# Blocks 5 to 15 of a dense layer taken in pairs, with 512-column first products

## The chip, the core and the metric

The kernel runs on one core of a Trainium2 chip. TensorE (PE, with its weight loads PEld), VectorE (DVE), ScalarE (ACT), GpSimd (POOL) and SyncE (SP, which issues most DMAs) run their own queues in order and wait for one another by semaphores. The metric is device time in microseconds of one execution. The kernel before took 1344.53 us, the median of three runs (1343.79 to 1345.99).

## The reference

Three layers on 4608 tokens, all in float32:

```python
# 1 chunked attention: 8 batches x 8 heads, 576 positions in 9 chunks of 64, head size 64
scores = 0.125 * q_c @ k_c.T;  attn = softmax(scores) (with + 1e-9 under the sum);  x = attn @ v_c
# 2 dense layer, 4608 x 512 -> 2048 -> 512
h = x @ w_in;  g = max(h, 0) + alpha * min(h, 0);  y = g @ w_out
# 3 eight experts, one for each token
logits = y @ w_gate;  e = argmax(logits);  p = max softmax(logits)
out = p * (max(y @ w1[e], 0) @ w2[e])
```

## The kernel before

The 4608 tokens are 36 tiles of 128, or 18 blocks of 256 (NB = 18, block j holds tiles 2j and 2j+1). Every float32 operand of the large products is kept as a high and a low part, and a product is three matmuls (high by high, and the two mixed ones).

The program has three stages. First the weights of the dense layer are brought into SBUF and the first blocks are started, in an order written out letter by letter (`ORDER`). Then a loop over steps (L963) runs the dense layer: one step is one block j and one m of 16 groups of 128 hidden units. Last come the experts, in 39 rounds of 128 rows (`m1`, `th`, `m2`).

A step of the dense layer is this. `mm1` (L334) makes h = 128 hidden units by 256 tokens, in 12 matmuls of 256 columns; the stationary operand is a piece of w_in, the moving one is the block's tokens. ACT makes r = max(-h, 0) (`g_r`, L357), DVE makes g from r, alpha and h (`g_x`, L362), ACT writes its high part (`g_h`, L366), POOL the low part (`g_l`, L370). `mm2` (L380), run three steps later, adds g by w_out onto y, in 6 matmuls of 512 columns. PSUM has eight banks: h0 and h1 for `mm1` in turn, y0 and y1 for the y of the block in work, a pair "s" for scores and a pair "o" for attention outputs and ranks.

Beside the steps stand, at places that two tables give by step (`bg`, after the products are issued, and `pre`, ahead of them):

- attention of a tile two to three blocks ahead, in a chain of ten steps (`CHAIN`): scores `at_s` (L200, 16 matmuls of 64x64, which the trace shows as 32), row maximum and its subtraction on DVE, exponentials on ACT (`soft_x`), sums (`soft_r`), a transpose on DVE (`at_tr`), the output `at_pv` (L313), and its high and low part written to the tokens (`at_xh`, `at_xl`). A chain starts every 8 steps, so that `at_pv` of one tile and `at_s` of the next stand in the same step, one behind the other.
- the gate of each finished tile: y is copied out (`gate_ev`, L404), eight dot products on DVE (`gate_l`, L416), maximum and one-hot (`gate_a`), an exponential (`gate_e`), a rank by two small matmuls (`gate_r`, L447 and L448), and the store of the row at its place (`gate_b`, a DMA issued by POOL).
- the split of the experts' weights, 128 pieces: a load into one of three buffers of `trio`, a high part on ACT and a low part on POOL into one of two others (`esplit`, L548, L479, L480), and a store to `wsp` in DRAM.

The order of the work on every engine is fixed by the program (`manual_schedule`); nothing is reordered by a scheduler.

Of the kernel before, what the change touches and what calls it, by code (L numbers as in the profile page):

```python
# [37 lines left out]
def tile_attention_moe(ctx, tc, q, k, v, w_in, w_out, alpha, w_gate, w1, w2, out):  # L38
# [76 lines left out]
    EARLY = 6  # L115
    EARLY_S = ("s", "o", "s", "o", "s", "s")
# [74 lines left out]
    pst, pp, xt = {}, {}, {}  # L191

    def at_s(i):
        j, tt = divmod(i, 2)
        s = pair(EARLY_S[i] if i < EARLY else "s", "s")[:, :, 0:256].rearrange("p h (a k) -> p h a k", a=4)
        for a in range(4):
            for c in range(2):
                for h in range(2):
                    r = slice(64 * h, 64 * h + 64)
                    nc.tensor.matmul(  # L200
                        out=s[64 * c:64 * c + 64, h, a],
                        lhsT=qs[j][r, a, 128 * tt + 64 * c:128 * tt + 64 * c + 64],
                        rhs=ks[j][r, 2 * tt + c, a],
                        start=True, stop=True,
                    )
        pst[i] = s
# [9 lines left out]
    def soft_b(i):  # L216
        s, mx = pst.pop(i), sm_t.pop(i)
        if i < 4:
            p = row_p.tile([128, ROW], F32, tag="row", name="p")[:, 0:512].rearrange("p (h k) -> p h k", h=8)
        else:  # L220
            p = at_p.tile([128, 8, 64], F32, tag="p", name="p")
# [40 lines left out]
    def soft_x(i, part):  # L262
        if part == 0:
            pp[i] = at_p.tile([128, 16, 32], F32, tag="p", name="px")
# [20 lines left out]
    def at_tr(i):  # L285
        p = pp.pop(i)
        ptb[i] = qk_p.tile([128, 4, 2, 64], F32, tag="ptt", name="ptt")
        nc.vector.transpose(out=ptb[i].rearrange("p a h (t k) -> p (a h t) k", t=2), in_=p)
# [3 lines left out]
    def at_pv(i):  # L292
        j, tt = divmod(i, 2)
        pt = ptb.pop(i)
        if i >= EARLY:
            o = pair("o", "o")[:, :, 0:256].rearrange("p c (a k) -> p c a k", a=4)
        elif i == 5:
            o = ot[4, 0][:, 1]
        else:
            ot[i, 0] = o = bank(EARLY_O[i], "o") if EARLY_O[i][0] in "yh" else pair(EARLY_O[i], "o")  # L300
            o = o if EARLY_O[i][0] in "yh" else o[:, 0]
        if i < EARLY:
            o = o.rearrange("p (a c k) -> p c a k", a=4, c=2)
        for a in range(4):
            for c in range(2):
                for h in range(2):
                    r = slice(64 * h, 64 * h + 64)
                    x = slice(64 * c, 64 * c + 64)
                    if i < EARLY:
                        lhs, rhs = vs[j].rearrange("p (x a k) -> p x a k", a=4, k=64)[r, 2 * tt + c, a], pt[r, a, c]  # L310
                    else:
                        lhs, rhs = vs[j].rearrange("p (x a h k) -> p x a h k", x=2, a=4, h=2)[x, tt, a, h], pt[x, a, h]
                    nc.tensor.matmul(out=o[r, c, a], lhsT=lhs, rhs=rhs, start=True, stop=True)  # L313
        if j not in xt:
            xt[j] = xt_p.tile([128, 2, 4, 256], F32R, tag="xt", name="xt")
        ot[i] = o

    def x_views(i):
        j, tt = divmod(i, 2)
        x = xt[j][:, :, :, 128 * tt:128 * tt + 128].rearrange("p n a (c k) -> p n c a k", c=2)  # L320
# [13 lines left out]
    def mm1(j, m):  # L334
        g4, mi = divmod(m, 4)
        h = hbank("h")[:, 0:256]
        w = W_in[g4]
        x = xt[j]
        n = 0
        for a in range(4):  # L340
            for wl, xl in ((0, 0), (0, 1), (1, 0)):
# [3 lines left out]
                    rhs=x[:, xl, a],  # L345
# [3 lines left out]
        hs_[j, m] = h  # L349
# [4 lines left out]
    def g_r(j, m):  # L354
        h = hs_.pop((j, m))
        r = tmp_p.tile([128, 256], F32, tag="r", name="r", bufs=3)
        nc.scalar.activation(out=r, in_=h, func=ACTF.Relu, scale=-1.0)  # L357
        rs[j, m] = r, h

    def g_x(j, m):  # L360
        r, h = rs[j, m]
        nc.vector.scalar_tensor_tensor(out=r, in0=r, scalar=calpha[:, m:m + 1], in1=h, op0=ALU.mult, op1=ALU.add)  # L362

    def g_h(j, m):
        gs[j, m] = g_p.tile([128, 2, 256], F32R, tag="g", name="g")
        nc.scalar.activation(out=gs[j, m][:, 0], in_=rs[j, m][0], func=ACTF.Copy)  # L366

    def g_l(j, m, eng=nc.gpsimd):
        g, r = gs[j, m], rs.pop((j, m))[0]
        eng.tensor_tensor(out=g[:, 1], in0=r, in1=g[:, 0].bitcast(F32), op=ALU.subtract)  # L370

    def g_a(j, m):
        g_r(j, m)
        g_x(j, m)

    def g_b(j, m):
        g_h(j, m)
        g_l(j, m)

    def mm2(j, m):  # L380
        g4, mi = divmod(m, 4)
        g = gs.pop((j, m))
        w = W_out[g4]
        if m == 0:
            if j == 1:
                y = pair("o", "y")
                ys[j] = [y[:, 0], y[:, 1]]
            else:
                ys[j] = [bank(f"y{t}", f"y{t}") for t in range(2)]
        for t in range(2):  # L390
            for n, (gl, wl) in enumerate(((0, 0), (0, 1), (1, 0))):
                nc.tensor.matmul(  # L392
                    out=ys[j][t],
                    lhsT=g[:, gl, 128 * t:128 * t + 128],
                    rhs=w[:, wl, mi],
                    start=(m == 0 and n == 0), stop=(m == MF - 1 and n == 2),
                )
# [80 lines left out]
    def split_piece(dst, raw, eng):  # L478
        nc.scalar.activation(out=dst[:, 0], in_=raw, func=ACTF.Copy)  # L479
        eng.tensor_tensor(out=dst[:, 1], in0=raw, in1=dst[:, 0].bitcast(F32), op=ALU.subtract)  # L480

# [11 lines left out]
    iu = trio[:, 0:2].rearrange("p a f -> p (a f)").bitcast(I32)  # L493
# [46 lines left out]
    def eload():  # L540
        if epieces:
            e, c, a = epieces.pop(0)
            t = sg_m()
            src = (w1[e, c, :, a, :] if c < 2 else w2[e, c - 2, :, a, :])
            nc.sync.dma_start(out=t, in_=src)
            eraw.append((e, c, a, t))

    def esplit():  # L548
        if eraw:
            e, c, a, t = eraw.pop(0)  # L550
            s = sg_u([128, 2, 512], "sp", F32R)
            split_piece(s, t, nc.gpsimd)
            nc.sync.dma_start(out=wsp[e, c, :, :, a, :].bitcast(F32), in_=s.bitcast(F32))
            eload()
# [7 lines left out]
    bg, pre = {}, {}  # L562
# [5 lines left out]
    order += [(j, m) for j in range(2, NB) for m in range(MF)]  # L568
# [6 lines left out]
    for j in range(4, NB):  # L575
        at(MF * (j - 2) + 4, load_qk, j)
        at(MF * (j - 2) + 12, load_v, j)
    for i in range(4):
        for d, e0, f in GATE0[i]:
# [14 lines left out]
    for i in range(4, NTILE - 2):  # L594
# [7 lines left out]
        at(s0 + r, gate_r, i)  # L602
        pre.setdefault(s0 + b, []).append((gate_b, (i,)))
    at(31, fill_rows)
    for x in range(3):
        at(32, eload)
    for x in range(len(epieces)):
        at(56 + 8 * x // 5, esplit)
# [4 lines left out]
    def early_count():  # L613
        c = pair("o", "cnt")[:, 0, 0:E]
# [42 lines left out]
    half, marks = {}, {}  # L657
    P2 = {}

    def open_p2():  # L660
        attn.close()
        st.enter_context(tc.tile_pool(name="xpad", bufs=1)).tile([128, 112], F32, name="xpad")
        for n, b in (("x2", 2), ("hx", 4), ("gi", 8), ("tb", 1)):
            P2[n] = st.enter_context(tc.tile_pool(name=n, bufs=b))

    def load(t):
        x = xg[t] = sg_m().rearrange("p (i f) -> p i f", i=4)
# [28 lines left out]
    def tx(t):  # L696
        xT[t] = P2["x2"].tile([128, 2, 4, 128], F32R, tag="xT", name="xT")
# [28 lines left out]
    def th(t, f):  # L726
        if f == 0:
            hT[t] = xt_p.tile([128, 2, 2, 4, 128], F32R, tag="xt", name="hT")
        blocks(hT[t][:, f], hx.pop((t, f)))

    def m2(t, f):
        if f == 0:
            yp[t] = bank(f"y{t % 2}", "y")
        passes(yp[t], hT[t][:, f], 2 + f, t, f == 0, f == 1)
        if f == 1:
            y = g_p.tile([128, 512], F32, tag="g", name="yo")
# [175 lines left out]
    for t in range(3):  # L912
# [6 lines left out]
        (mm2, NB - 1, MF - 1), (gate_ev, a), (gate_l, a, 0, 4), (gate_ev, b), (gate_l, a, 4, 8), (gate_l, b, 0, 1),  # L919
# [16 lines left out]
    with tc.manual_schedule():  # L936
# [5 lines left out]
        def by_step(f):  # L942
            return lambda x, *e: f(*order[x], *e)

        def hook(d):
# [3 lines left out]
            Q=load_part_qk, I=iload, G=lambda _: load_wgb(), V=load_v, N=lambda _: nc.sync.dma_start(out=calpha, in_=alpha), K=load_qk,  # L949
# [6 lines left out]
        for t in ORDER.split():  # L956
            e = t[-1:]
            if e in engs:
                ops[t[0]](int(t[1:-1]), engs[e])
            else:  # L960
                ops[t[0]](int(t[1:]))
        done = 30
        for s in range(32, NS):  # L963
            j, m = order[s]
            hooks(pre, s)
            g_b(*order[s - 1])
            mm1(j, m)
# [84 lines left out]
```

## Time and profile before

| | |
|---|---|
| median of three runs | 1344.53 us |
| the profiled execution: its own time, its span | 1346.69 us, 1344.7 us |
| PE busy | 1317.9 us (98%) |
| weight loads busy | 1155.1 us (86%) |
| DVE, ACT, POOL busy | 980.0, 738.2, 690.1 us |
| mean granted TensorE clock | 0.995 |

The span is from the first to the last instruction. A busy PE is not PE at its peak: matmuls overlap, so that a matmul of 256 columns shows as 0.28 us but the next starts 0.12 us behind it. What a group of matmuls costs is read from the starts of the groups around it. In a row of the timeline the first figure is the start, the second the length up to the end of the last of the group, which overlaps the next.

### The profile page before, as it was taken

What the parts mean: (1) busy time and instruction counts of PE and PEld (TensorE: products, weight loads), DVE (VectorE), ACT (ScalarE), POOL (GpSimd) and SP (SyncE); (2) the same over time, 40 slices, a digit from 0 to 9 for tenths busy, and PEclk for the clock granted to TensorE, in tenths of its full rate; (3) what the DMA queues carried; (4) which work ended last, traced back from release to release, by engine and by line L of the source; (5) the groups of instructions that cost most, each with busy time, mean ns of one, the idle gap of its engine ahead of it and who ended that gap; (6) DMA issues with size and microseconds to landing.
All of it is one profiled execution on the core that took longest, in us unless ns stands there. A gap on an engine that the chain in (4) does not pass through costs nothing. (4 is left out here: it accounts for less than half of the span.)

```text
span 1344.7 us, 29901 instructions
## 1 busy us (share of the span) xinstructions
PE 1317.9 (98%) x9561; PEld 1155.1 (86%) x9561; DVE 980.0 (73%) x2489; ACT 738.2 (55%) x1961; POOL 690.1 (51%) x725
## 2 busy tenths in 40 slices
PE   7999999999999999999999999999899999999997
PEld 7898899999999999999999999887688888888885
DVE  6887877878877877887887786568966666665653
ACT  4654554555555555455555554339576665566663
POOL 3322336667666665765766664334354444444442
PEclk8999999999999999999999999999999999999999
DMA  9154414666656666566665661285125416966670
GB/s 373 68 173 152 119 61 162 218 213 201 220 194 207 217 214 222 184 219 214 201 220 193 207 217 68 69 300 235 48 68 177 173 49 255 333 215 220 217 282 35
DMA packets 107872, 249.07 MB, mean 185 GB/s; under 512 B 15104, under 2 KB 36096, under 8 KB 102592
## 3 DMA queue, kind: packets, MB, share of 16 engines
q1 hardware_dynamic: 101712, 227.37, 49.9%
q0 software_dynamic: 6000, 19.70, 3.9%
q8 instruction: 84, 1.38, 0.4%
q14 instruction: 76, 0.62, 0.1%
HBM read 401.39 MB, written 88.91 MB: 365 GB/s over the span
## 5 line engine op out<-in xcount | busy, mean ns | idle before, releaser
L342 PEld LDWEIGHTS h<-xt,ring 128*128 128x128 f32 x3456 | 452.4, 191 | 23.3
L342 PE MATMUL h<-xt,ring 128*128 128x256 f32 x3456 | 459.9, 283 | 0.0
L392 PE MATMUL y<-ring,g 128*128 128x512 f32 x1728 | 452.1, 397 | 0.0
L392 PEld LDWEIGHTS y<-ring,g 128*128 128x128 f32 x1728 | 305.8, 189 | 53.3 <-ACT g L366 0.2
L370 POOL TENSOR_TENSOR g<-r,g 128x256 fp32r<-128x256 f32 x279 | 241.1, 865 | 201.7 <-ACT g L366 199.1
L416 DVE CUSTOM_DVE_ANT_0 junk<-row,wgb 128x512 bf16<-128x512 f32 x288 | 257.0, 892 | 8.1 <-ACT row L404 3.8
L362 DVE SCALAR_TENSOR_TENSOR r<-r,calpha,h 128x256 f32<-128x256 f32 x288 | 137.2, 476 | 171.4 <-ACT r L357 170.7
L480 POOL TENSOR_TENSOR sp<-trio,sp 128x512 fp32r<-128x512 f32 x128 | 179.5, 1402 | 106.2 <-ACT sp L479 99.4
L724 DVE TENSOR_SCALAR hx<-h 32x128 f32<-32x128 f32 x576 | 165.3, 287 | 89.9 <-PE h L706 82.5
L357 ACT ACTIVATE r<-h 128x256 f32<-128x256 f32 x288 | 110.5, 384 | 217.7 <-PE h L342 177.4
L706 PE MATMUL y<-ring,hT 128*128 (+1 forms) x936 | 220.5, 390 | 5.3 <-POOL hT L694 3.1
L706 PE MATMUL h<-ring,xT 128*128 (+1 forms) x936 | 219.1, 389 | 2.1 <-DMA ring<-wsp 1.7
L694 POOL TENSOR_TENSOR hT<-z,hT 128x512 fp32r<-128x512 f32 x78 | 100.7, 1308 | 220.8 <-ACT hT L693 220.7
L706 PEld LDWEIGHTS y<-ring,hT 128*128 128x128 f32 x936 | 175.0, 188 | 44.5 <-POOL hT L694 5.0
L706 PEld LDWEIGHTS h<-ring,xT 128*128 128x128 f32 x936 | 175.4, 188 | 39.1 <-issue 2.1
L366 ACT ACTIVATE g<-r 128x256 fp32r<-128x256 f32 x288 | 119.5, 415 | 133.1 <-PE y L392 107.8
L722 ACT ACTIVATE hx<-h 32x128 f32<-32x128 f32 x672 | 179.5, 267 | 10.3 <-PE h L706 2.8
L693 ACT ACTIVATE hT<-z 128x512 fp32r<-128x512 f32 x78 | 48.0, 633 | 115.4 <-DVE z L691 111.2
L271 ACT ACTIVATE px<-s 32x256 f32<-32x256 f32 x240 | 89.7, 374 | 3.8 <-DVE s L260 1.0
L479 ACT ACTIVATE sp<-trio 128x512 fp32r<-128x512 f32 x128 | 80.5, 629 | 1.1 <-DMA wsp<-sp 0.5
L691 DVE STREAM_TRANSPOSE z<-trio 128x512 f32<-128x512 f32 x39 | 27.6, 707 | 47.4 <-POOL hT L694 47.4
L694 POOL TENSOR_TENSOR xT<-z,xT 128x512 fp32r<-128x512 f32 x39 | 51.7, 1326 | 16.1 <-ACT xT L693 15.5
(166 smaller groups left out, 909.6 us busy)
## 6 DMA issues: line engine op xcount, KB each, us to landing
ring<-wsp SPq DMA_DIRECT2D x70, 4096.0 KB
wsp<-sp SPq DMA_DIRECT2D x128, 512.0 KB
trio<-in_w SPq DMA_DIRECT2D x128, 256.0 KB
ring<-wsp SPq DMA_DIRECT2D x8, 2048.0 KB
trio<-xs SPq DMA_DIRECT2D x156, 64.0 KB
vt<-in_v SPq DMA_DIRECT2D x18, 512.0 KB
qt<-in_q SPq DMA_DIRECT2D x17, 512.0 KB
kt<-in_k SPq DMA_DIRECT2D x17, 512.0 KB
```

Of the source, the lines that this page charges most:

```text
L342: nc.tensor.matmul(out=h, lhsT=w[:, wl, a, 128 * mi:128 * mi + 128], rhs=x[:, xl, a], start=(n == 0), stop=(n == 11),)
L357: nc.scalar.activation(out=r, in_=h, func=ACTF.Relu, scale=-1.0)
L362: nc.vector.scalar_tensor_tensor(out=r, in0=r, scalar=calpha[:, m:m + 1], in1=h, op0=ALU.mult, op1=ALU.add)
L366: nc.scalar.activation(out=gs[j, m][:, 0], in_=rs[j, m][0], func=ACTF.Copy)
L370: eng.tensor_tensor(out=g[:, 1], in0=r, in1=g[:, 0].bitcast(F32), op=ALU.subtract)
L392: nc.tensor.matmul(out=ys[j][t], lhsT=g[:, gl, 128 * t:128 * t + 128], rhs=w[:, wl, mi], start=(m == 0 and n == 0), stop=(m == MF - 1 and ...
L416: nc.vector.tensor_tensor_reduce(out=junk, in0=r[:, 0:512], in1=wgb[e // 2][:, e % 2], scale=1.0, scalar=0.0, op0=ALU.mult, op1=ALU.add, a ...
L480: eng.tensor_tensor(out=dst[:, 1], in0=raw, in1=dst[:, 0].bitcast(F32), op=ALU.subtract)
L694: nc.gpsimd.tensor_tensor(out=dst[:, 1], in0=z, in1=dst[:, 0].bitcast(F32), op=ALU.subtract)
L706: ins.append(nc.tensor.matmul(out=out, lhsT=lhs[:, xl, a], rhs=w[:, rows_, wl, a], start=(first and a == 0 and n == 0), stop=(last and a = ...
L722: nc.scalar.activation(out=dst, in_=src, func=ACTF.Relu)
L724: V.tensor_scalar(out=dst, in0=src, scalar1=0.0, scalar2=None, op0=ALU.max)
```

## The change

From the middle of block 5 to the middle of block 15, two blocks go through one `mm1` together: 12 matmuls of 512 columns for the two, each a whole bank of h, where there were two times 12 of 256. The pairs overlap by halves: blocks 5 and 6 share m = 8 to 15, blocks 6 and 7 share m = 0 to 7, blocks 7 and 8 share m = 8 to 15, and so on. There are 80 such double steps (10 pairs of blocks, 8 values of m). `g_r`, `g_x`, `g_h` and `g_l` work on 512 columns; `mm2` keeps its matmuls, 12 for the two blocks, two double steps later.

What this needs is moved too. The tokens stand in one tile of three places (`XT`, block j at j mod 3), g and r in two buffers of 512 columns each. Blocks with even j from 6 on have their y in the pair "o", so that ranks and attention outputs of that stage go to the pair "s", which the scores use as well. In the double steps the chain of a tile (`LONE`) takes a cycle of four of them: `at_s` after the products of one, `at_pv` after the products of another, hence apart; before them, up to tile 13, chains start every 6 or 7 steps (`begin`). Gates have tables of their own (`PAIRED`): two dot products each double step, ranks up to eight steps later. q, k and v are loaded by tile and no longer by block. Expert pieces are split in place, in three buffers in turn.

```diff
-    for i in range(6, NTILE):
-        for d, f, *part in CHAIN:
-            at(max(8 * (i - 2) - 5, 30) + d, f, i, *part)
...
+    for j in range(JOIN, LAST + 1):
+        steps += [((j - 1, j), m) for m in (range(HALF, MF) if (j - JOIN) % 2 == 0 else range(HALF))]
...
+    LONE = (
+        (post, 1, at_s), (own, 2, soft_a), (own, 2, soft_s), (own, 2, soft_x, 0), (bg, 2, soft_x, 1), (own, 4, soft_r), (own, 6, at_tr),
+        (post, 7, at_pv), (own, 8, at_xh), (own, 8, at_xl),
+    )
+    n = 2 * JOIN + 2
+    begin = {i: 30 + (WIDE - 43) * (i - EARLY) // (n - 1 - EARLY) if i < n else WIDE - 2 + 8 * (i - n) for i in range(EARLY, NTILE)}
...
+        if i + 1 < NTILE:
+            at(begin[i] + 2, tile_qk, i + 1)
+            at(begin[i] + 9, tile_v, i + 1)
...
-    def mm1(j, m):
+    def mm1(*js, m):
         g4, mi = divmod(m, 4)
-        h = hbank("h")[:, 0:256]
+        h = hbank("h")[:, 0:256 * len(js)]
...
-                    rhs=x[:, xl, a],
+                    rhs=XT[:, xl, a, y],
...
-            if j == 1:
+                if j == 1 or j >= JOIN and j % 2 == 0:
...
-            rk = pair("o", "rk")[:, 0, 0:E]
+            rk = pair("o" if i < 2 * JOIN - 4 else "s", "rk")[:, 0, 0:E]
...
+    PAIRED = (
...
+        ((4, 0, 2), (6, 2, 4), (8, 4, 6), (10, 6, 8), (14, 19, 20)),
+        ((12, 0, 2), (14, 2, 4), (16, 4, 6), (18, 6, 8), (22, 27, 28)),
...
+    def esplit(n):
+        eload()
+        done = [eraw.pop(0) for _ in range(n)]
+        for e, c, a, t in done:
+            nc.scalar.activation(out=t[:, 0].bitcast(F32R), in_=t[:, 1], func=ACTF.Copy)
+            nc.gpsimd.tensor_tensor(out=t[:, 1].bitcast(F32R), in0=t[:, 1], in1=t[:, 0], op=ALU.subtract)
...
+        for js, m in steps:
+            n = len(js)
+            for x in range(n):
+                hooks(pre, s + x)
+            g_b(*todo[-1][1], m=todo[-1][2])
+            for x in range(n):
+                hooks(own, s + x)
+            mm1(*js, m=m)
+            g_a(*js, m=m)
+            for x in range(n):
+                hooks(bg, s + x)
+            while todo[0][0] + 2 + len(todo[0][1]) <= s:
+                _, a, b = todo.pop(0)
+                mm2(*a, m=b)
+            for x in range(n):
+                hooks(post, s + x)
```

PE in the middle of the dense layer, before (o is an attention output, s are scores, h the first product, y the second):

```order
L342 MATMUL h<-xt,ring_911 128x256 x12
L313 MATMUL o<-ptt,vt 64x64 x16
L200 MATMUL s<-kt,qt 64x64 x16
L392 MATMUL y_7018<-ring_911,g 128x512 x3
L392 MATMUL y_7019<-ring_911,g 128x512 x3
L342 MATMUL h<-xt,ring_911 128x256 x12
```

PE at the same kind of place in the changed kernel, from a rank (rk) to the second product behind the scores:

```order
L475 MATMUL rk<-ohsum,ones 128x8
L366 MATMUL h<-xt,ring_885 128x512 x12
L418 MATMUL y_4328<-ring_885,g 128x512 x3
L418 MATMUL y_4329<-ring_885,g 128x512 x3
L418 MATMUL y<-ring_885,g 128x512 x6
L323 MATMUL o<-pt_1490,vtile 64x64 x16
L366 MATMUL h<-xt,ring_885 128x512 x12
L418 MATMUL y_4328<-ring_885,g 128x512 x3
L418 MATMUL y_4329<-ring_885,g 128x512 x3
L418 MATMUL y<-ring_885,g 128x512 x6
L211 MATMUL s<-qkt 64x64 x16
L366 MATMUL h<-xt,ring_72 128x512 x12
```

The output of one tile and the scores of the next, which stood together between a first and a second product, now stand apart, each between a second and a first product. In the order of before the pair stands together for all 30 tiles from 6 on; in that of the changed kernel it does so at two places.

DVE ahead of an attention output, before (the transpose into ptt is what `at_pv` waits for):

```order
L362 SCALAR_TENSOR_TENSOR r<-r,calpha,h 128x256
L462 TENSOR_SCALAR se<-se 128x1
L463 RECIPROCAL row<-se 128x1
L467 ISA rkt,pos<-rk,oh 128x8
L467 ISA pos 128x1
L468 CAST posi<-pos 128x1
L470 TENSOR_TENSOR ohsum<-ohsum,oh 128x8
L362 SCALAR_TENSOR_TENSOR r<-r,calpha,h 128x256
L288 STREAM_TRANSPOSE ptt<-px 128x512
```

DVE at the same kind of place in the changed kernel:

```order
L443 ISA junk,lg<-row,wgb 128x512
L443 ISA lg 128x1
L489 TENSOR_SCALAR se<-se 128x1
L490 RECIPROCAL row<-se 128x1
L494 ISA rkt,pos<-rk,oh 128x8
L494 ISA pos 128x1
L495 CAST posi<-pos 128x1
L497 TENSOR_TENSOR ohsum<-ohsum,oh 128x8
L298 STREAM_TRANSPOSE pt_1490<-pt_1490 128x512
L386 SCALAR_TENSOR_TENSOR r<-r,calpha,h 128x512
L443 ISA junk,lg<-row,wgb 128x512
```

Here the rank of a tile is read and the transpose follows in the same double step whose products `at_pv` stands behind; ahead of them are two dot products of the double step before.

## Rows read from the trace of the kernel before

**Rows 1.** PE's waits over the whole run: us in total, times, longest

```profile
PE y L706 <- POOL hT L694: 3.1, 4, 1.1
...
PE rk L447 <- DVE pos L467: 0.2, 1, 0.2
```

**Rows 2.** Busy us of each engine by window; then PEclk, DMA share, GB/s

```profile
250.00:850.00 600.00, 599.96 (x5218) 541.89 (x5218) 471.15 (x1161) 316.93 (x812) 384.62 (x393) 1.00 0.60 197
```

**Rows 3.** Timeline of PE, 600 to 606 us: start, length, line, tiles, shape, count

```profile
600.07 1.60 PE L342 MATMUL h<-xt,ring 128*128 128x256 f32 x12
601.50 1.55 PE L392 MATMUL y<-ring,g 128*128 128x512 f32 x6
602.89 1.60 PE L342 MATMUL h<-xt,ring 128*128 128x256 f32 x12
```

**Rows 4.** Timeline of PE in the experts' stage, 1100 to 1112 us

```profile
1100.29 5.60 PE L706 MATMUL h<-ring,xT 128*128 x24
...
1111.16 1.07 PE L706 MATMUL h<-ring,xT 128*128 x4
```

**Rows 5.** Timeline of PE, 41 to 48.5 us, early in the first stage

```profile
41.62 1.66 PE L392 MATMUL y<-ring,g 128*128 128x512 f32 x6
43.21 1.15 PE L313 MATMUL o<-pt,vt 64*64 64x64 f32 x32
44.29 3.01 PE L392 MATMUL y<-ring,g 128*128 128x512 f32 x12
47.14 1.59 PE L342 MATMUL h<-xt,ring 128*128 128x256 f32 x12
```

**Rows 6.** Timeline of PE, 162 to 168.5 us: output and scores together

```profile
163.56 1.59 PE L342 MATMUL h<-xt,ring 128*128 128x256 f32 x12
...
165.60 0.65 PE L200 MATMUL s<-kt,qt 64*64 64x64 f32 x32
...
167.67 1.12 PE L342 MATMUL h<-xt,ring 128*128 128x256 f32 x8
```

**Rows 7.** Timeline of PE, 138.5 to 154 us: scores alone

```profile
139.19 1.59 PE L342 MATMUL h<-xt,ring 128*128 128x256 f32 x12
140.71 0.69 PE L200 MATMUL s<-kt,qt 64*64 64x64 f32 x32
141.34 1.66 PE L392 MATMUL y<-ring,g 128*128 128x512 f32 x6
142.83 1.59 PE L342 MATMUL h<-xt,ring 128*128 128x256 f32 x12
```

**Rows 8.** Timeline of PE around two ranks, 158 to 163.5 and 895 to 912 us

```profile
157.75 1.59 PE L342 MATMUL h<-xt,ring 128*128 128x256 f32 x12
...
160.73 1.60 PE L342 MATMUL h<-xt,ring 128*128 128x256 f32 x12
...
895.87 0.18 PE L447 MATMUL rk<-oh,tri 128*128 128x8 f16 x1
...
895.94 5.75 PE L392 MATMUL y<-ring,g 128*128 128x512 f32 x24
901.52 8.32 PE L706 MATMUL h<-ring,xT 128*128 128x512 f32 x36
```

**Rows 9.** Costliest groups, 400 to 800 us: busy, mean ns, idle before

```profile
L416 DVE CUSTOM_DVE_ANT_0 junk<-row,wgb 128x512 bf16<-128x512 f32 x134 | 127.4, 951 | 1.7
L480 POOL TENSOR_TENSOR sp<-trio,sp 128x512 fp32r<-128x512 f32 x84 | 117.9, 1404 | 69.2 <-ACT sp L479 64.5 <-ACT g L366 2.8
...
L362 DVE SCALAR_TENSOR_TENSOR r<-r,calpha,h 128x256 f32<-128x256 f32 x134 | 63.7, 475 | 76.0 <-ACT r L357 75.8
...
L428 DVE SCALAR_TENSOR_TENSOR key<-lg,gmx,desc 128x8 f32<-128x8 f32 x17 | 32.5, 1911 | 0.6
...
L288 DVE STREAM_TRANSPOSE ptt<-px 128x512 f32<-128x512 f32 x17 | 11.9, 701 | 0.0
L260 DVE TENSOR_TENSOR s<-s,mx 128x512 f32<-128x512 f32 x17 | 11.9, 700 | 0.6
```

More of the change, by code (lines that the diff above doesn't have):

```diff
@@ L217, in soft_b @@
         s, mx = pst.pop(i), sm_t.pop(i)
[L218 to L221, printed above, removed]
+        p = row_p.tile([128, ROW], F32, tag="row", name="p")[:, 0:512].rearrange("p (h k) -> p h k", h=8)
         nc.vector.tensor_tensor(
@@ L263, in soft_x @@
         if part == 0:
-            pp[i] = at_p.tile([128, 16, 32], F32, tag="p", name="px")
+            if not pt2:
+                pt2.append(at_p.tile([128, 2, 512], F32, tag="pt", name="pt2"))
+            pp[i] = pt2[0][:, 0].rearrange("p (x k) -> p x k", x=16)
         s = pst[i].rearrange("p h a (e k) -> p e a h k", e=2)
@@ L376, in g_b, with g_h, g_l, g_a @@
[L376 to L380, printed above, removed]
+    def g_h(*js, m):
+        gs[js, m] = slot(G, 0, js)
+        nc.scalar.activation(out=gs[js, m][:, 0], in_=rs[js, m][0], func=ACTF.Copy)
+    def g_l(*js, m, eng=nc.gpsimd):
+        g, r = gs[js, m], rs.pop((js, m))[0]
+        eng.tensor_tensor(out=g[:, 1], in0=r, in1=g[:, 0].bitcast(F32), op=ALU.subtract)
+    def g_a(*js, m):
+        g_r(*js, m=m)
+        g_x(*js, m=m)
+    def g_b(*js, m):
+        g_h(*js, m=m)
+        g_l(*js, m=m)
@@ L381, in mm2 @@
+    def mm2(*js, m):
         g4, mi = divmod(m, 4)
-        g = gs.pop((j, m))
+        g = gs.pop((js, m))
         w = W_out[g4]
-        if m == 0:
-            if j == 1:
[L386 to L397, printed above, removed]
+        for x, j in enumerate(sides(*js)):
+            if j not in ys:
+                if j == 1 or j >= JOIN and j % 2 == 0:
+                    y = pair("o", "y")
+                    ys[j] = [y[:, 0], y[:, 1]]
+                else:
+                    ys[j] = [bank(f"y{t}", f"y{t}") for t in range(2)]
+                fed[j] = 0
+            for t in range(2):
+                for n, (gl, wl) in enumerate(((0, 0), (0, 1), (1, 0))):
+                    nc.tensor.matmul(
+                        out=ys[j][t],
+                        lhsT=g[:, gl, 256 * x + 128 * t:256 * x + 128 * t + 128],
+                        rhs=w[:, wl, mi],
+                        start=(fed[j] == 0 and n == 0), stop=(fed[j] == MF - 1 and n == 2),
+                    )
+            fed[j] += 1
@@ L567, in tile_attention_moe @@
     order = [(j, 4 * g + m) for g in range(4) for j in range(2) for m in range(4)]
-    order += [(j, m) for j in range(2, NB) for m in range(MF)]
+    HALF = MF // 2
+    WIDE = MF * JOIN - HALF
+    steps = [((j,), m) for j in range(2, JOIN - 1) for m in range(MF)] + [((JOIN - 1,), m) for m in range(HALF)]
+    for j in range(JOIN, LAST + 1):
+        steps += [((j - 1, j), m) for m in (range(HALF, MF) if (j - JOIN) % 2 == 0 else range(HALF))]
+    steps += [((LAST,), m) for m in (range(HALF) if (LAST - JOIN) % 2 == 0 else range(HALF, MF))]
+    steps += [((j,), m) for j in range(LAST + 1, NB) for m in range(MF)]
+    ends = {j: MF * (j + 1) + (HALF if JOIN - 1 <= j < LAST else 0) for j in range(NB)}
     CHAIN = (
@@ L593, in tile_attention_moe @@
     )
-    for i in range(4, NTILE - 2):
+    PAIRED = (
[5 rows of a table added]
+    )
+    for i in range(2 * JOIN - 4, 2 * LAST):
+        s0 = ends[i // 2]
+        late_ = 2 * JOIN - 2 <= i < 2 * LAST - 6
+        pre.setdefault(s0 + (4 if s0 % MF else 3), []).append((gate_ev, (i,)))
+        *parts, (a, r, b) = PAIRED[4 if i == 2 * LAST - 7 else i % 2 + 2 * late_]
+        for d, e0, e1 in parts:
+            at(s0 + d, gate_l, i, e0, e1)
+        own.setdefault(s0 + a, []).append((gate_a, (i,)))
+        at(s0 + a, gate_e, i)
+        post.setdefault(s0 + r, []).append((gate_r, (i,)))
+        pre.setdefault(s0 + b, []).append((gate_b, (i,)))
+    for i in [*range(4, 2 * JOIN - 4), *range(2 * LAST, NTILE - 2)]:
         s0 = MF * (i // 2 + 1)
@@ L601, in tile_attention_moe @@
         at(s0 + a + 1, gate_e, i)
[L602 to L605, printed above, removed]
+        r, b = rank_at(i, s0 + r, s0 + (r + 1 if i < 2 * JOIN - 4 else b))
+        at(r, gate_r, i)
+        pre.setdefault(b, []).append((gate_b, (i,)))
+    at(34, fill_rows)
+    for x in range(2):
         at(32, eload)
     for x in range(len(epieces)):
-        at(56 + 8 * x // 5, esplit)
+        own.setdefault(56 + 8 * x // 5, []).append((esplit, (1,)))
+    for s in range(WIDE, MF * (LAST + 1) - HALF, 2):
+        n = sum(len([x for x in own.get(t, []) if x[0] is esplit]) for t in (s, s + 1))
+        for t in (s, s + 1):
+            own[t] = [x for x in own.get(t, []) if x[0] is not esplit]
+        if n:
+            own[s].insert(0, (esplit, (n,)))
     cnt = {}
@@ L657, in tile_attention_moe @@
     half, marks = {}, {}
+    yo = []
     P2 = {}
@@ L942, in by_step @@
         def by_step(f):
-            return lambda x, *e: f(*order[x], *e)
+            return lambda x, **e: f(order[x][0], m=order[x][1], **e)
         def hook(d):
```

169 lines of the change are left out of this document (92 added, 77 removed), and 3 rows, old and new, of the table PAIRED.

## The prediction

> **What bounds the kernel now.** I read the list of PE's waits first. The reader is to see how little stands in it for the dense layer: after the first stage, and until the experts begin, PE waited once, for a rank, 0.2 us; the longer entries, like 3.1 us on POOL, are of the stages around it [rows 1]. The windows say the same from the other side: from 250 to 850 us PE is busy for 599.96 of 600 us at a granted clock of 1.00 (the 2.4 GHz level), DVE for 471 and POOL for 385 [rows 2]. So in the stage that the change touches, time is what PE's own matmuls take, one behind the other, and the change is priced by PE's order alone, as long as no wait is made. The timeline of PE gives the prices, by the starts of neighbouring groups.
>
> A step takes 602.89 - 600.07 = 2.82 us: 1.43 for twelve 256-column matmuls (120 ns each) and 1.39 for six of 512 columns (231 ns each) [rows 3]. In the experts' stage, where all have 512 columns, 48 in a row take 1111.16 - 1100.29 = 10.87 us, 226.5 ns each [rows 4]. A matmul of 256 columns thus costs more than half of one with 512; that is what the change can win. What stands between the products is dear beyond its own length, since the matmul ahead of it and those behind it are slower. That is what the change can lose.
>
> **The change part by part.**
>
> *Double steps.* Two steps of before are 5.64 us. A double step is 24 matmuls of 512 columns, with all neighbours of 512 columns too, so I price it from the experts' rows: 5.435 us [rows 4]. The second product wins as well, since its 231 ns belong to the mixed order: where twelve second products followed each other, they took 47.14 - 44.29 = 2.85 us, of which the first six behind an insertion took 1.49 (142.83 - 141.34) and so the other six 1.36, or 227 each [rows 5, 7]. Gain 0.205 us, times 80: **-16.4 us**. Bounds: if wide products stayed at 231 ns, 24 would take 5.55 us and the gain is 7.2; if one wide cost two narrow ones (240 ns), the first product wins nothing. I take 226.5, the row with the same neighbours.
>
> The Trainium skill speaks against the change here. Its page "TensorE: Matmul & The Clock Gate", in the section "Back-to-back issue gap", gives a warm gap of columns / 2.4 + about 2.5 ns, which is 109 ns at 256 columns and 216 at 512: by it, 960 mergings would save 2.5 us and no more, and with the losses below the kernel would be slower, near 1354 us. The trace has 120 and 226.5 ns [rows 3, 4], some 13 ns over the columns at both widths, and does not agree; I go by the trace.
>
> *Attention apart.* Before, output and scores stand together and cost 167.67 - 163.56 - 2.82 = 1.29 us per tile over a plain step [rows 6]. Apart, in the double steps, each insertion costs three things: its own 32 matmuls, 141.34 - 140.71 = 0.63 us [rows 7]; the twelve matmuls behind it, 2.85 where 2.72 is plain (half of 5.435), 0.13 [rows 4, 5]; and a longer last matmul ahead of it, since six second products with insertions on both sides took 43.21 - 41.62 = 1.59 and with one only ahead 1.49, 0.10 [rows 5, 7]. That is 0.86, for output and scores 1.72, so 0.43 more per tile. The order has 20 scores and 20 outputs directly ahead of a wide product: **+8.6 us**. Bounds: nothing more than together (0), if the streams of 512 columns hid the slow start; 0.89, if the loss around each (0.13 + 0.10) were twice that, for which no row speaks (behind a rank, the nearest, 5.58 - 5.435 = 0.145 over 24 matmuls [rows 8]). I take the middle, the rows as they are. The other 8 tiles that come apart stand among narrow steps, where one alone costs 142.83 - 139.19 - 2.82 = 0.82 [rows 7]: 1.64 against 1.29, 0.35 each: **+2.8 us**.
>
> *Ranks.* Before, 160.73 - 157.75 - 2.82 = 0.16 us. Ahead of 24 matmuls of 512 columns it is 0.07 for the rank itself and 5.58 - 5.435 = 0.145 behind it, 0.215 [rows 8]. There are 19 such: **+1.0 us**.
>
> Sum: -16.4 + 8.6 + 2.8 + 1.0 = **-4.0 us**. Against the profiled execution that is 1342.7 for its 1346.69 us, which was 2.2 over the median of the runs; from the median, 1344.53 - 4.0 = **1340.5 us**.
>
> *What I cost at nothing, and its cover.* The other engines get less to do: a DVE pass over 512 columns takes about 0.70 us (the subtraction of the maxima) against two of 0.475 [rows 9], which saves 1.0 us of DVE in each cycle of four double steps; DVE goes from 79% of the stage [rows 2] to some 76%. So the question is waits, not load. Four are new or tighter.
> (1) A bank of h is free again when `g_x` has read it; from the end of one wide product to the next use of its bank lie a wide product and two second products, 8.2 us. Worst case: scores' maxima and their subtraction (2 x 0.70), four exponentials, relu and `g_x`, all behind the dot products left over; this ends some 7 us after the double step's start, and the bank is wanted at 11.
> (2) The first of PE's 24 matmuls on a reused y waits for two copies of y on ACT, issued ahead of a wide product of 2.72 us, which is about twice their length.
> (3) `at_pv` waits for DVE's transpose in the same double step. What stands ahead on DVE's queue: `g_x` (0.70, not before relu, 3.4 us into the step before), two dot products (2 x 0.95) that run some 0.6 us into this double step, the rank's six short instructions, and the transpose (0.70) [rows 9]. Done by 2.7 us, wanted at 5.4. Behind a late transpose stand `g_x` and both dot products, and PE waits itself.
> (4) `at_s` of the next tile waits until the outputs have been read out of the shared pair "s": ACT and DVE have a double step for it, for some 1.4 us of work.
> SP's queue gets 2 more kinds of load per tile and is passed by none that waits long: q and k are asked for behind the scores that free their buffer, some three double steps before use, v likewise. Expert pieces go round in three buffers, 14 us a turn at 1.25 pieces per double step, of which ACT and POOL take about 2 us (1.40 on POOL [rows 9]); the rest is for a store and a load. The experts' stage and the first 130 us keep their order. Any of these gone wrong costs what PE then waits; no row of before prices it, from zero (nothing is there to win, PE did not wait) to several tenths per tile.
>
> **The rivals.**
> *B, the hand-over stalls (slower).* Place: `at_pv` behind DVE's transpose, wait (3). For it: a DVE instruction on eight values took 1.91 us in the mean and a dot product 0.95 [rows 9], where they are short of work, so DVE's instructions stretch beside POOL, and POOL's become longer (1.40 for 512 columns). Against: 2.7 us of slack, and before no wait with an equally busy DVE [rows 1, 2]. Price: it decides above 2.7 us of delay; 0.2 us of wait at each of 20 tiles eats the gain, 0.4 makes 8 us, 1348.5.
> *C, given back at the change of stage.* If what PE waits for when the experts begin (3.1 us on POOL for transposed rows, among others [rows 1]) is set by other engines and not by PE's arrival, those 4 us become waits: 1344.5, no change. Against: the gates of the last tiles hang on PE's last products.
> *D, wide products as dear as two narrow ones (slower).* At 231 ns the sum is -7.2 + 12.4 = +5.2, 1349.7; at 240 ns, where only the second product gains (12 x 4.5 ns x 80 = 4.3), +8, 1352.6. Against: 48 matmuls at 226.5 with the same kind of weight loads [rows 4]. The Trainium skill's gap, above, is of this kind, with 1354.
> *E, insertions among wide products cost no more apart than together.* Then -16.4 + 2.8 + 1.0 = -12.6, 1331.9. For it: two of the three terms come from the first stage. Against: the same 0.1 us in each row [rows 5 to 8].
>
> **How the numbers follow.** Forecast, within 1.5 us of the sum: 0.54. B 0.20, C 0.14, D 0.07, E 0.05. A difference of 0.2% (2.7 us) is about what a measurement of this kernel can tell from none. Faster by more: the forecast but for 0.04, and E: 0.55. Within: C, those 0.04 and 0.06 of B with small waits: 0.24. Slower: the rest of B, and D: 0.21. The range is 1336.5 to 1348.5: up to B's price, down to about half-way to E, the forecast's own being 1339 to 1342.
>
> **What would show it.** In the changed kernel's timeline: 24 matmuls between double steps in 5.44 us (5.55 or more: D); rows of outputs and scores with 0.86 each around them (0.65: E); a list of PE's waits still empty in the dense layer, `at_pv` on DVE's transpose being the entry to look for (B); the experts' first matmul 4 us earlier, at 897.5, and the end too (the first without the second: C). The forecast is wrong if PE waits for over 1.5 us in the dense layer or if a double step misses 5.44 by more than 0.02.

## The result and the profile after

The changed kernel is slower: 1358.13 us (median of 4 runs, 1354.62 to 1360.46) against 1344.68 for the kernel before on the same chip, a ratio of 1.0097 (95% interval 1.0073 to 1.0121). The forecast was 1340.5, the range ended at 1348.5. The profiled execution took 1358.76 us, 12.1 more than before's 1346.69.

I read it in the order of the prediction. First PE's waits, 132 to 905 us, the stretch in which before had one wait of 0.2 us [rows 1] (us in total, times, longest):

```profile
PE rk L474 <- DVE lg L458: 5.5, 4, 4.0
PE h L366 <- DVE r L386: 3.1, 5, 1.1
PE rk L474 <- DVE oh L457: 2.2, 2, 1.9
PE rk L474 <- ACT pt L281: 2.0, 1, 2.0
PE rk L474 <- DVE pos L494: 0.8, 1, 0.8
PE y L418 <- ACT row L431: 0.3, 1, 0.3
```

The sum is 13.9 us, and 10.5 of it stand at `rk`, the rank, which the prediction's list of waits didn't hold at all. `at_pv`, the place that rival B named, is missing from it.

Next the windows, with before's columns [rows 2]: the middle is as full as before, both ends of the paired stretch are not.

```profile
300.00:350.00 50.00, 45.37 (x284) 36.24 (x284) 32.21 (x84) 21.11 (x46) 28.31 (x24) 0.93 0.66 211
...
550.00:600.00 50.00, 50.00 (x338) 40.17 (x337) 39.70 (x91) 26.22 (x56) 28.48 (x25) 1.00 0.67 222
...
700.00:750.00 50.00, 46.17 (x319) 36.89 (x319) 39.78 (x90) 21.50 (x46) 29.85 (x25) 1.00 0.58 194
```

One cycle of four double steps in that full middle, on PE's timeline; it answers to [rows 3], [rows 6] and [rows 8]:

```profile
604.29 0.18 PE L474 MATMUL rk<-oh,tri 128*128 128x8 f16 x1
...
607.16 2.88 PE L418 MATMUL y<-ring,g 128*128 128x512 f32 x12
609.97 0.69 PE L323 MATMUL o<-pt,vtile 64*64 64x64 f32 x32
610.60 3.02 PE L366 MATMUL h<-xt,ring 128*128 128x512 f32 x12
613.45 2.88 PE L418 MATMUL y<-ring,g 128*128 128x512 f32 x12
...
619.75 2.88 PE L418 MATMUL y<-ring,g 128*128 128x512 f32 x12
...
625.19 2.88 PE L418 MATMUL y<-ring,g 128*128 128x512 f32 x12
627.91 0.18 PE L474 MATMUL rk<-oh,tri 128*128 128x8 f16 x1
```

An undisturbed double step (619.75 to 625.19) takes 5.44 us, as forecast. The output costs 610.60 - 609.97 = 0.63 for itself, the products ahead 2.81 and behind 2.85 where 2.72 is plain: 0.85 in all, 0.86 forecast. A rank costs 0.06 for itself and 0.09 at the product behind it, 0.15 against 0.215. The cycle, rank to rank, is 23.62 us; before's was 24.02 (585.95 to 609.97 us of its timeline). The gain is 0.40 us a cycle; the prediction's terms give (-16.4 + 8.6 + 1.0) / 20 = -0.34.

Now the largest hole, on PE's timeline:

```profile
311.18 2.88 PE L418 MATMUL y<-ring,g 128*128 128x512 f32 x12
318.08 0.17 PE L474 MATMUL rk<-oh,tri 128*128 128x8 f16 x1 [4.02 <-DVE lg L458]
...
318.14 5.27 PE L366 MATMUL h<-xt,ring 128*128 128x512 f32 x12
323.24 1.98 PE L418 MATMUL y<-ring,g 128*128 128x512 f32 x8
```

The rank stands behind the second product of its double step and waits 4.02 us for the one-hot (L457; the list names L458, the instruction right behind it). From the start of the last product to that of the rank it is 4.4 us; "hole" means this distance below. Behind the rank the first product takes 5.10 us (323.24 - 318.14), where behind a rank in the middle it took 2.81 (607.16 - 604.35): the window 316.2 to 323 us has the granted clock at 0.50, the 1.2 GHz level, against 1.00 on both sides of it.

```profile
311.00:316.00 5.00, 3.06 (x14) 2.21 (x12) 4.86 (x11) 2.98 (x6) 2.56 (x2) 1.00 0.78 271
316.20:323.00 6.80, 4.92 (x14) 3.88 (x15) 3.56 (x14) 1.46 (x4) 4.33 (x4) 0.50 0.81 265
323.00:330.00 7.00, 7.00 (x61) 5.56 (x60) 3.45 (x8) 2.44 (x5) 2.90 (x3) 1.00 0.52 150
```

Why the one-hot is late, from the timelines of SP's queue, ACT, DVE and POOL (put in that order), read from the top:

```profile
304.62 0.33 SPq L568 DMA_DIRECT2D sp<-in_w  x1
...
307.89 0.63 ACT L575 ACTIVATE sp<-sp 128x512 fp32r<-128x512 f32 x1 [3.83 <-DMA sp<-in_w]
308.43 1.52 ACT L281 ACTIVATE pt<-s 32x256 f32<-32x256 f32 x4
...
310.61 0.75 DVE L386 SCALAR_TENSOR_TENSOR r<-r,calpha,h 128x512 f32<-128x512 f32 x1 [4.83 <-ACT r L381]
...
313.33 2.50 DVE L290 COPY st<-sr 32x16 f32<-32x16 f32 x4
...
317.70 0.23 DVE L457 TENSOR_SCALAR oh<-key,km 128x8 f16<-128x8 f32 x1
...
312.87 1.30 POOL L394 TENSOR_TENSOR g<-r,g 128x512 fp32r<-128x512 f32 x1 [2.99 <-ACT g L390]
314.18 1.26 POOL L576 TENSOR_TENSOR sp<-sp 128x512 fp32r<-128x512 f32 x1
```

An expert piece is asked for only at 304.62, when the store of its buffer has landed. ACT stands 3.83 us at the piece's split, with the exponentials and the relu queued behind it. DVE idles 4.83 us for that relu, works off its queue, among it four tiny copies that take 2.50 us beside POOL, and reaches the one-hot at 317.7.

Why the piece is late, from POOL and SP's queue, and from SP's list of waits for 250 to 320 us:

```profile
295.04 1.30 POOL L576 TENSOR_TENSOR sp<-sp 128x512 fp32r<-128x512 f32 x1 [0.94 <-PE y L418]
...
300.02 0.33 SPq L568 DMA_DIRECT2D sp<-in_w  x1
300.40 0.54 SPq L578 DMA_DIRECT2D wsp<-sp  x1
...
SPq L568 <- DMA wsp<-sp: 44.4, 13, 4.6
```

POOL has finished a piece at 296.3, but its store leaves at 300.40: on SP's queue it stands behind the load of 300.02, which waits until the store before has landed. The load of 304.62 waits for this store in turn, and so the loads leave 4.5 to 4.6 us apart (290.91, 295.51, 300.02, 304.62), one behind each store. The count of such waits alone says little: run 7, in which ACT waits for no piece here, still has 12 (34.4 us), but most of its stores leave as soon as POOL is done.

Last, the experts' stage. It begins 12.2 us later than before's 901.52 [rows 8], and the execution ends 12.1 later:

```profile
913.73 8.32 PE L785 MATMUL h<-ring,xt 128*128 128x512 f32 x36
```

So the loss lies in the dense layer, at the two ends of the paired stretch. Against the forecast's 897.5 for the experts' first matmul the gap is 16.2 us: 13.9 of waits and 2.3 of half clock add up to 16.2. The sum hides one thing: the first stage, up to the scores at 128.87 us, ended 2.5 us sooner in this execution than in before's (131.39), so as much excess lies in short stretches that I did not list one by one (1.3 of it in scores and products at half clock around 130 us, where before and run 8 had the full clock).

### The profile page after: what moved, and what is told of

Same layout as the page of the kernel before. It is cut to its first block, busy times and chain, and to the rows that moved or that the text cites. A ratio compares the mean times of both kernels' runs of the same rounds, so it can differ in the third digit from the quotient of the medians.

```text
span 1357.0 us, 27575 instructions
## 1 busy us (share of the span) xinstructions
PE 1316.3 (97%) x8601; PEld 1100.3 (81%) x8601; DVE 968.6 (71%) x2409; ACT 715.4 (53%) x1801; POOL 656.2 (48%) x645
## 5 line engine op out<-in xcount | busy, mean ns | idle before, releaser
L366 PE MATMUL h<-xt,ring 128*128 128x256 f32 (+1 forms) x2496 | 445.8, 328 | 3.1 <-DVE r L386 3.1
L394 POOL TENSOR_TENSOR g<-r,g 128x256 fp32r<-128x256 f32 (+1 forms) x199 | 212.8, 1072 | 300.1 <-ACT g L390 234.2
L773 POOL TENSOR_TENSOR xt<-z,xt 128x512 fp32r<-128x512 f32 x117 | 152.0, 1314 | 238.5 <-ACT xt L772 237.9
L386 DVE SCALAR_TENSOR_TENSOR r<-r,calpha,h 128x256 f32<-128x256 f32 (+1 forms) x208 | 119.4, 574 | 174.6 <-ACT r L381 173.2
L785 PE MATMUL y<-ring,xt 128*128 (+1 forms) x936 | 220.7, 390 | 5.3 <-POOL xt L773 3.0
L785 PE MATMUL h<-ring,xt 128*128 (+1 forms) x936 | 219.2, 390 | 2.1 <-DMA ring<-wsp 1.7
L785 PEld LDWEIGHTS y<-ring,xt 128*128 128x128 f32 x936 | 174.9, 188 | 44.7 <-POOL xt L773 5.3
L785 PEld LDWEIGHTS h<-ring,xt 128*128 128x128 f32 x936 | 175.4, 188 | 39.2 <-issue 2.1
L390 ACT ACTIVATE g<-r 128x256 fp32r<-128x256 f32 (+1 forms) x208 | 103.7, 499 | 163.2 <-PE y L418 84.5
L576 POOL TENSOR_TENSOR sp<-sp 128x512 fp32r<-128x512 f32 x128 | 170.5, 1338 | 8.3 <-ACT sp L575 7.3
```

The source lines that it names most:

```text
L366: nc.tensor.matmul(out=h, lhsT=w[:, wl, a, 128 * mi:128 * mi + 128], rhs=XT[:, xl, a, y], start=(n == 0), stop=(n == 11),)
L390: nc.scalar.activation(out=gs[js, m][:, 0], in_=rs[js, m][0], func=ACTF.Copy)
L576: nc.gpsimd.tensor_tensor(out=t[:, 1].bitcast(F32R), in0=t[:, 1], in1=t[:, 0], op=ALU.subtract)
L773: nc.gpsimd.tensor_tensor(out=dst[:, 1], in0=z, in1=dst[:, 0].bitcast(F32), op=ALU.subtract)
L785: ins.append(nc.tensor.matmul(out=out, lhsT=lhs[:, xl, a], rhs=w[:, rows_, wl, a], start=(first and a == 0 and n == 0), stop=(last and a = ...
```

## The experiments

Each was timed in five rounds beside the kernel before (medians 1345.3 to 1346.0); ratios are to it, with their 95% intervals.

**1. Rank at the front.** The theory at first, R: the early rank. At the ends of the stretch `PAIRED` puts rank and one-hot (`gate_a`) into the same double step, in the middle five steps apart (the expectations say eight), two double steps; so the ends wait. Tiles 8 and 9 get the middle's entry. (Expert pieces have three buffers in the changed kernel, not the two of which the expectations speak.)

```
-        late_ = 2 * JOIN - 2 <= i < 2 * LAST - 6
+        late_ = i < 2 * LAST - 6
```

> One edit of the changed kernel: tiles 8 and 9, the first two of the paired stretch, get the late rank too (gates over four double steps, rank eight steps behind the one-hot of its tile). Theory R (a rank that stands in the same double step as the one-hot it reads waits for VectorE): the waits at 314 us (4.4 us) and 344 us (0.8 us) go, and with the first of them the half clock behind it (about 2.2 us): 7 us less than the changed kernel, about 1351. The waits at 717 to 861 us stay. Theory L (the loads of expert pieces, with two buffers of which each is stored before it is loaded again, make ScalarE and so VectorE late around 310 us, whatever waits for them): TensorE meets the same lateness at the first product's bank (g_x) or at the attention output, and the time moves by less than 2 us, 1356 to 1359.

Measured: 1355.32 us, 1.0084 (1.0070 to 1.0098), under half of what R expects, and the two intervals overlap. The hole moved to the next insertion, the attention output. The list names no releaser ("issue"); DVE's transpose ended 0.1 us before it, at 320.90. The slow matmuls came along (the nine shown took 3.74 us):

```profile
321.00 0.69 PE L323 MATMUL o<-pt,vtile 64*64 64x64 f32 x32 [2.06 <-issue]
321.63 3.74 PE L366 MATMUL h<-xt,ring 128*128 128x512 f32 x9
```

So DVE is late there whatever waits for it: the rank is not the cause by itself.

**2. Rank at both ends, first try.**

```
-        *parts, (a, r, b) = PAIRED[4 if i == 2 * LAST - 7 else i % 2 + 2 * late_]
+        *parts, (a, r, b) = PAIRED[i % 2 + 2 * (i < 2 * LAST - 4)]
+        if i == 2 * LAST - 3:
+            r, b = 22, 23
+        if i == 2 * LAST - 2:
+            r, b = 15, 16
```

> The changed kernel with the late rank at both ends of the paired stretch (tiles 8 to 27; tile 28's rank four steps behind its one-hot). Theory R: all eight rank waits of the changed kernel go (about 12 us) and the half clock with the first (2.2 us), at a few tenths of a microsecond for waits elsewhere: 12 to 14 us less than the changed kernel, 1344 to 1347, level with the kernel before. Theory L: the lateness moves to the bank of the first product, 1353 to 1358.

Measured: 1356.46, 1.0077 (1.0063 to 1.0091). A flaw of mine: the ranks of tiles 25 and 26 fell into one step, and the second waited 3.4 us (from 767 us on) until DVE had read the first (`pos`, L494). It tells little; run 6 mends it. (By the edit tiles 8 to 25 have the late rank, not 8 to 27.)

**3. Splits behind the relu** in the unpaired steps (`esplit` moved from the own part of a step to its background).

```
+    for t in list(own):
+        if not WIDE <= t < MF * (LAST + 1) - HALF:
+            n = [x for x in own[t] if x[0] is esplit]
+            own[t] = [x for x in own[t] if x[0] is not esplit]
+            for x in n:
+                at(t, *x[0:1], *x[1])
```

> The changed kernel with the expert pieces' splits (ScalarE) of the unpaired steps issued behind the relu of their step, not ahead of it; the buffers stay two. Theory L: ScalarE no longer holds the exponentials behind a piece that has not landed, the wait at 314 us and its half clock go (6 to 7 us), the waits from 717 us on stay: about 1351. Theory R: the one-hot of tile 8 is a few tenths earlier at best, since VectorE's own queue (2.5 us of small copies beside GpSimd) stands ahead of it; 1 to 3 us less, 1355 to 1357.

Measured: 1357.58, 1.0091 (1.0077 to 1.0105), level with the changed kernel, and the wait at 314 us is still there (4.39 us between starts). The split that held ACT, for 3.82 us here, belongs to the first double step, which this edit leaves alone. It doesn't speak against the pieces; it missed the one that matters.

**4. No late rank anywhere** (`late_ = False`).

> The reverse edit: the changed kernel with no late rank at all (tiles 10 to 20 as the ends: gates within two double steps, rank in the double step of its one-hot). Theory R: the middle tiles now wait as the ends do, 1 to 4 us at each of most of the 11 tiles, 10 to 30 us more than the changed kernel (1368 to 1388), more where the clock drops behind a wait. Theory L: the middle has a split only every other double step and its pieces have long landed; no more than 3 us more (1358 to 1361).

Measured: 1366.42, 1.0162 (1.0148 to 1.0177). The tiles that lose the late rank are 10 to 23. Each now waits, but little. PE's waits from 380 to 700 us in this run:

```profile
PE rk L474 <- DVE lg L458: 4.3, 13, 0.4
```

0.33 us each, in the same order that costs 4.0 at 314 us. From rank to rank a cycle takes 24.12 us here ((683.57 - 394.14) / 12 by the timeline), 23.62 in the changed kernel. So the early rank is worth 0.5 us a tile; what makes it 4 at the front is something else that meets it there. This is theory J: piece and rank together. The front hole itself grew in this run, the rank's wait to 6.8 us, with ACT waiting 6.05 us for its piece in place of 3.83; that is a part of the 8 us by which the total is longer.

**5. Fewer pieces ahead of the stretch**, ranks untouched; and with run 2's purpose added.

```
-        own.setdefault(56 + 8 * x // 5, []).append((esplit, (1,)))
+        own.setdefault(56 + 2 * x if x < 16 else 88 + 20 * (x - 16) // 13, []).append((esplit, (1,)))
```

> The changed kernel with fewer expert pieces ahead of the paired stretch: one every two steps (16 of them) where it was one every 1.6, and the rest spread evenly behind. Ranks as in the changed kernel. Theory J (two conditions meet at 314 us: ScalarE is held by a piece that has not landed, 3.8 us, so VectorE is late with the one-hot, and the rank is the first to stand behind it): with the piece landed in time the rank at 314 us waits under 1 us and the clock stays up, 5 to 6 us less than the changed kernel, 1351 to 1353; the waits from 717 us on stay. Theory R alone (VectorE's own queue, whatever ScalarE does): the wait stays at 3 us or more, 1356 to 1359.

> Both edits: all ranks late and the slower pieces. Theory J: no wait over 1.5 us is left between 300 and 860 us and the clock stays up: 11 to 13 us less than the changed kernel, 1345 to 1347, still no gain on the kernel before worth naming, since waits of the first product at 221, 272 and 835 to 841 us are left. Theory L or R alone: one of the two edits does nothing, and this equals the better single one (1349 to 1353).

Measured: 1365.25, 1.0152 (1.0139 to 1.0165), and 1357.91, 1.0089 (1.0074 to 1.0103). Both totals miss, for a reason in my edit: it moved the later pieces as well, and in the middle the scores now wait for the shared pair "s", wait (4) of the prediction (run 7, which leaves the later pieces alone, has no such wait). In the first of them, 132 to 905 us:

```profile
PE s L211 <- DVE xt L337: 9.2, 8, 2.0
```

At the front, though, J held: the rank's wait at 314 us was 1.44 us in the first and none in the second, both without a drop of the clock.

**6. Late ranks for all, the last ones spread** (run 2 mended), pieces as in the changed kernel.

```
+        *parts, (a, r, b) = PAIRED[i % 2 + 2 * (i < 2 * LAST - 2)]
+        if i >= 2 * LAST - 3:
+            r, b = {2 * LAST - 3: (25, 26), 2 * LAST - 2: (17, 18), 2 * LAST - 1: (21, 22)}[i]
```

> The late rank for all paired tiles, with the ranks of the last four tiles set so that each stands at least four steps behind the one before (in the earlier run two ranks of neighbouring tiles fell into one step at 767 us, and the second waited 3.4 us for the first one's sum). Pieces as in the changed kernel. Theory J: the front wait moves to the attention output (2.5 us and its half clock stay, as in the run with the front alone), the rank waits from 717 us on go: 3 less at the front and 5 to 7 less at the end, 1349 to 1351. If VectorE's lag at the end shows at the first product's bank: 1353 to 1356.

Measured: 1351.19, 1.0042 (1.0029 to 1.0055), 7 us under the changed kernel. What is left, 132 to 905 us:

```profile
PE h L366 <- DVE r L386: 3.7, 4, 1.6
PE o L323 <- issue: 2.7, 1, 2.7
PE rk L474 <- DVE pos L494: 2.2, 1, 2.2
```

The output's wait is the front hole again, with a drop of the clock behind it; ACT waited 5.65 us for a piece there.

**7. The pieces alone, cleanly:** from step 48 on one every two steps, every later one where it was.

```
+        own.setdefault(48 + 2 * x if x < 20 else 56 + 8 * x // 5, []).append((esplit, (1,)))
```

> The changed kernel with the 20 expert pieces ahead of the paired stretch issued one every two steps, from step 48 on, and every later piece in the step that it has in the changed kernel (the slower run before this had moved those too, and new waits of the scores' transfer buffer came in the middle). Ranks as in the changed kernel. Theory J (the piece that has not landed makes VectorE late, and the early rank waits for VectorE): the rank at 314 us waits 1 to 2 us without a drop of the clock, the rest stays: 4 to 5 us less than the changed kernel, 1353 to 1354. Rival (early rank alone): 1357 to 1360.

Measured: 1353.11, 1.0053 (1.0040 to 1.0066), as J says. ACT no longer waits for a piece there, the rank waits for a third as long (1.44 us, 4.02 before the edit), and the product behind it runs at full clock:

```profile
316.34 0.17 PE L474 MATMUL rk<-oh,tri 128*128 128x8 f16 x1 [1.44 <-DVE lg L458]
...
316.39 2.99 PE L366 MATMUL h<-xt,ring 128*128 128x512 f32 x12
```

**8. Pieces and ranks** (the edits of 6 and 7).

> Late ranks for all paired tiles, and the pieces ahead of the stretch one every two steps from step 48, later ones where they were. Theory J: the wait of the attention output at 320 us (2.7 us with the slow matmuls behind it) goes, 4 us less than late ranks alone: 1346 to 1348, the waits at 222, 274, 817, 834 and 851 us stay. Rival: VectorE's queue alone holds the attention output there, 1350 to 1352.

Measured: 1347.44, 1.0007 (0.9998 to 1.0016): the two edits bring the excess over the kernel before from 13.4 us down to 1.5 (1347.44 against 1345.95 beside it), and the two kernels are level. The attention output behind which run 6 lost its 2.7 us now follows at once:

```profile
319.08 0.69 PE L323 MATMUL o<-pt,vtile 64*64 64x64 f32 x32
319.70 3.02 PE L366 MATMUL h<-xt,ring 128*128 128x512 f32 x12
```

The waits left, 132 to 905 us, are 5.9 us, nearly all near the stretch's end and behind it (812, 828 and 845 us):

```profile
PE rk L474 <- DVE pos L494: 2.8, 2, 2.2
PE h L366 <- DVE r L386: 2.5, 3, 1.6
PE rk L475 <- DVE ohsum L497: 0.6, 1, 0.6
```

**9. The price of attention apart.** The changed kernel with the scores right behind the output of the tile before; a pair "s" holds both, in two column halves.

```
+            both.append(pair("s", "so"))
...
+            o = both[0][:, :, 256:512] if both else pair("o", "o")[:, :, 0:256]
...
+                when.setdefault(begin[i] + (-1 if f is at_s and i > n else d), []).append((f, (i, *part)))
```

> One edit of the changed kernel, at the term of the prediction for small matmuls placed apart: the scores of a tile go right behind the attention output of the tile before, as one group of 32 small matmuls among the wide products in place of two of 16 (scores and outputs of the stretch share one PSUM pair, in two column halves). By the prediction's price (0.43 us for a tile whose two groups stand apart, 17 tiles): 7 us less, about 1351, if the waits of the changed kernel stay as they are. If a group's neighbours cost nothing: 1356 to 1359.

Measured: 1355.44, 1.0079 (1.0067 to 1.0092). The total is diluted, since the waits did not stay: the first rank's grew from 4.0 to 6.8 us, as in run 4, and here too ACT waited longer for the piece, 6.22 us. The middle tells the price:

```profile
583.37 0.69 PE L327 MATMUL so<-pt,vtile 64*64 64x64 f32 x32
583.88 0.65 PE L213 MATMUL so<-qkt 64*64 64x64 f32 x32
...
606.60 0.69 PE L327 MATMUL so<-pt,vtile 64*64 64x64 f32 x32
```

A cycle is 606.60 - 583.37 = 23.23 us, 0.39 less than apart (23.62), where the prediction took 0.43.

**10. All three edits** (8 and 9).

> The same with scores and attention outputs as one group of small matmuls (0.37 us a tile measured in the middle of the adjacent run, 5.5 us over 15 tiles): 5 to 7 us less than the same without it, 1340 to 1342, under the kernel before. If the wider group makes VectorE's and ScalarE's work collide elsewhere: 1344 to 1348.

Measured: 1341.22, 0.9958 (0.9943 to 0.9973): faster than both kernels, than the one before by 4.7 us in the medians and 5.7 by the ratio. Its seven runs spread from 1337.20 to 1344.87.

## Why the prediction was wrong

*The sum on PE was right.* Double steps, insertions and their neighbours came out as priced (5.44, 0.85 against 0.86), apart against together as 0.39 against 0.43, the cycle as -0.40 against -0.34. D fails at the 5.44, E at the 0.85, C at the experts' stage, which ends as much later as it begins. The gap rule behind the prediction's other price for D fails too: the double step took 5.44 / 24 = 227 ns a matmul, not 216. In the Trainium skill, page "TensorE: Matmul & The Clock Gate", section "Back-to-back issue gap", that rule is the gap of an isolated matmul; for a stream of weight loads and matmuls the section gives about 131 ns at 512 columns, and this trace doesn't agree with that either.

*The step that failed is "What I cost at nothing, and its cover".* Four waits stand there, and the fifth, the rank behind the one-hot, doesn't. Its place could be read from the table: eight tiles at the ends (8, 9 and 24 to 29) have `gate_a` and `gate_r` in one double step, the middle ones don't. I priced the rank as an insertion (19 x (0.215 - 0.16) = 1.0) and never asked what it waits for. In the changed kernel the ranks waited 10.5 us in all, and with late ranks (run 6) 2.2. Run 4 prices the wait where nothing else is late at 0.5 us a tile.

*The same step's sentences on the pieces and on SP's queue failed as well.* "Three buffers, 14 us a turn" is right for the paired stretch: from 400 to 700 us ACT's splits start 4.69 us apart, 14.1 a turn, and there ACT hardly waits. The turn is no shorter ahead of the stretch (the splits from 202.77 to 303.45 are 5.0 us apart, and 4.8 in the kernel before), so the rate alone doesn't explain the delay. What the sentence left out is the order on SP's queue, of which the prediction said that none that waits long stands in it: a load that waits for a store holds up the next store. Why the queue fell behind ahead of the stretch and not in it, no run separates. Run 7 shows the pieces' part at the front, run 6 that late ranks alone leave that hole, run 8 that both together close it.

*The waits cost more than themselves.* The prediction had no term for the clock: behind the hole of 4.4 us at 314 us the half clock cost another 2.3 us.

*Rival B* had the right sign and engine (DVE's small instructions beside POOL) and the wrong place. Such instructions did get longer: the four copies ahead of a transpose took 0.8 us before and 2.6 after, by their means from 400 to 800 us (before's row first):

```profile
L280 DVE COPY st<-sr 32x16 f32<-32x16 f32 x64 | 12.9, 202 | 1.2
L290 DVE COPY st<-sr 32x16 f32<-32x16 f32 x68 | 44.1, 648 | 1.3
```

`at_pv` on the transpose came only in runs 1, 2 and 6, after the rank had been moved out of its way.

*At the end of the stretch* the waits of 2.0 and 1.9 us at 719 and 727 us are two different ones: the first rank (tile 23, one double step behind its one-hot) shares its pair with scores of the double step before and waits for their exponentials (`ACT pt`), the second waits for a one-hot behind four copies that took 3.73 us. Late ranks remove both (run 6).

With the waits and the slow clock taken out, the forecast holds. In run 8, whose clock stays up, it is 772.0 us from the last scores of the first stage to the experts' first product (130.17 to 902.19 us), 766.1 without its 5.9 us of waits. The kernel before took 770.1 (131.39 to 901.52): 4.0 more, as forecast.

## What to carry to other kernels

When a step gets longer and its engines wider, list for every instruction of the bottleneck engine, the tiny ones too, what it waits for and how long ago that was issued; a matmul of 8 columns held PE for 4 us. Check the table's first and last entries apart from its middle: the loss lay there, and the middle was as good as planned. Where buffers are loaded, used and stored in turn, count the order of the queue that issues the transfers too: a load that waits for a store also holds up the store behind it, and buffers times interval does not show that.

## What the runs showed of the hardware

PE's granted clock fell to 0.50 after the hole of 4.4 us, and 12 matmuls took 5.10 us instead of 2.81. The length of a hole doesn't settle it: a wait of 1.74 us at 858 us in the second kernel of run 5 was followed by a drop (0.51 from 860 to 863.5 us), one of 2.17 at 845 us in run 8 by none. Two holes of 2.3 us close together, at 717 and 724 us, were followed by no drop in the changed kernel and by one in run 7 (nine matmuls from 724.2 to 727.5 us):

```profile
710.00:728.00 18.00, 14.17 (x94) 11.07 (x93) 15.19 (x42) 8.12 (x20) 9.18 (x7) 1.00 0.64 222
```

```profile
724.20:727.50 3.30, 3.30 (x9) 2.60 (x8) 0.39 (x1) 0.91 (x2) 3.27 (x3) 0.50 0.44 148
```

Four DVE copies of 32 x 16 took 0.70 us where POOL was idle, and 2.48 where it subtracted (run 6, at 220 and 316 us):

```profile
220.02 0.70 DVE L290 COPY st<-sr 32x16 f32<-32x16 f32 x4
...
315.95 2.48 DVE L290 COPY st<-sr 32x16 f32<-32x16 f32 x4
```
